# Moving pair 1's K transposes, a value load and a copy in the front of an attention and MLP kernel

## The chip, the cores and the metric

The kernel runs on one core of one Trainium2 chip. The metric is the device time of one execution in microseconds (us). The kernel before takes 340.07 us, the median of three runs (339.52 to 340.18).

The engines are TensorE (PE in the profile; PEld is its weight load), VectorE (DVE), ScalarE (ACT), GpSimd (POOL) and SyncE (SP). Each runs its own instructions in the order in which they were written, and waits on semaphores for the others. GpSimd and SyncE also issue the transfers (DMAs).

## The reference

Inputs are q, k and v with 8 batches, 8 heads, 576 positions and a head dimension of 64, a forget gate f per batch, head and position, and the two weights of an MLP (512 to 2048 to 512).

```python
scores = scale * np.matmul(q, k.transpose(0, 1, 3, 2))
log_f = np.log(np.clip(f, 0.0001, 1.0))
cum = np.cumsum(log_f, axis=-1)
decay = cum[:, :, :, None] - cum[:, :, None, :]
scores = np.where(causal, -1000000000.0, scores + decay)
attn = softmax(scores)          # written out in the reference
x = (attn @ v)                  # heads side by side: 4608 tokens of 512
h = x @ w_in
out = (h - np.tanh(h)) @ w_out
```

So each head has causal attention with a decay that is the difference of two running sums, and an MLP with the activation h - tanh(h) follows.

## The kernel before

**Pairs and tiles.** The work of attention is cut into 32 pairs of heads (4 pairs in each of 8 batches; pair 0 holds heads 0 and 1 of batch 0, pair 1 heads 2 and 3, and so on). A pair has seven score tiles (`TILES`), numbered 0 to 6. Tiles 0, 1, 2 are the first head's keys 0 to 511, tiles 4, 5, 6 the second head's. Tile 3, the tail tile, holds the last 64 keys of both heads: two small matmuls, one for each head. Scores are computed keys by queries, by `scores` (line 337): a matmul at line 352 from the transposed K (`KT`) and the transposed Q (`QT`), for batch 0 a second one at line 355 that adds the causal mask (`late`), and an exp on ScalarE (line 361). The decay is inside the matmul: `KT` and `QT` have 67 rows, 64 of the head dimension and 3 of the decay (constants, a high half `chi` and a low half `clo` of the running sum).

**The decay rows.** They are computed once: ScalarE takes the logarithm (line 184), VectorE the running sum (line 187), `chi` (line 189) and `clo` (line 190). For head 0 they are written directly. For heads 1 to 7 of batch 0 three DMAs on GpSimd's queue, at the top of `bulk` (lines 211 to 213: K's chi, Q's chi, K's clo), bring them into `KT` and `QT`.

**Loads.** Q, K and V are loaded on GpSimd's queue, with a cast to fp16: before `bulk` the first four heads of Q and K (lines 149 to 152, line 102), the last 64 positions of V (`load_v_rest`, line 123) and V of heads 0 and 1 (`load_v_head`, line 127, one DMA for each head); then the mask is made on GpSimd (line 169). `bulk` issues the decay rows, Q and K of heads 4 and 5, Q and K of heads 6 and 7, and V of heads 2 to 7 in four blocks (line 131). A DMA on this queue takes one of eight semaphores in turn, and so waits until the eighth before it has landed. Loads of batch 1 and of the weights (`load_win`, line 222, `load_wout`, line 226) follow from the table `LOADS` as the pairs go on.

**Transposes.** `trans` (line 287) turns a pair's Q or K on TensorE: six small transposes into one bank of the accumulator memory (line 298), and then two copies into `QT` or `KT`, even positions and odd positions. The string `copies` names the engine of each copy: "VV" puts both on VectorE (line 311), "AV" the first on ScalarE (line 309) and the second on VectorE. For pair 0 each copy is cut in two again.

**Banks.** Scores use the pool `ps_sc` (two banks in turn), and some of them the pool `ps_tr`, which has one bank, `tr`. In pair 0 the tail tile uses `tr`; in pair 1 tiles 0, 3 and 6 do. Transposes of the first pairs use three further banks in turn.

**Unread matmuls.** `unread(n)` (line 563) issues n matmuls of 128 columns whose result nobody reads, by default into `tr`.

**Order.** The order on each engine is written out by hand. `start` does pair 0's transposes and its tiles 0 and 1; `bulk` follows; then `att_items(p)` lists pair p's work, tile by tile. For pair 0: after the scores of tile 1 the transposes of pair 1's Q, after tile 2 six unread matmuls, after the scores of tile 3 the transposes of pair 1's K, after tile 5 four unread matmuls and after tile 6 six. During pair p the next pair's Q and K are turned (at `at_q` and `at_k`, line 614) and the values of the pair before are computed (`values`, line 382: the matmul of the exps with V at line 389, the first head at tile 2, the second at tile 4), divided on VectorE (lines 398 to 400). From pair 4 on matmuls of the MLP (line 451 and, later, 492 and 517) are mixed in. From batch 1 on the causal mask is applied by GpSimd behind the exp (line 371).

Of the kernel before, what the change touches and what calls it, by code (L numbers as in the profile page):

```python
# [21 lines left out]
def kernel(  # L22
# [18 lines left out]
    NPAIR = H // 2  # L41
# [51 lines left out]
    qn, kn = ([t[0:S // NT6, :].rearrange("p (h n d) -> p h n d", h=H, n=NT6) for t in raw] for raw in (qraw, kraw))  # L93
# [3 lines left out]
    KT = [qkp.tile([D + 3, H, PITCH], FP16, tag=f"KT{i}", name=f"KT{i}") for i in range(2)]  # L97
# [3 lines left out]
    def load_qk(dst, src, b, h0, h1):  # L101
        nc.gpsimd.dma_start(  # L102
            out=dst[b % 2][:, h0:h1, :, :].rearrange("p h n d -> p h (n d)"),
            in_=src[b, h0:h1, :, :].rearrange("h (p n) d -> p h (n d)", n=NT6))
# [21 lines left out]
    def load_v_head(b, h):  # L126
        nc.gpsimd.dma_start(out=vn[b % 2][:, 0:NJ - 1, h, 0:D],  # L127
                            in_=v[b, h, 0:S - S % P, :].rearrange("(n p) d -> p n d", p=P))

    def load_v_block(b, n, h0, h1):  # L130
        nc.gpsimd.dma_start(out=vn[b % 2][:, n, h0:h1, 0:D],  # L131
                            in_=v[b, h0:h1, n * P:(n + 1) * P, :].rearrange("h p d -> p h d"))
# [32 lines left out]
    EL = [cst.tile([P, 192], FP16, tag=f"el{i}", name=f"el{i}") for i in range(3)]  # L165
    load_v_rest(0)
    load_v_head(0, 0)
    load_v_head(0, 1)
    nc.gpsimd.affine_select(out=late, in_=late, compare_op=ALU.is_ge, fill=-60000.0,
                            base=0, pattern=[[1, P]], channel_multiplier=-1)  # L170

# [21 lines left out]
    def aug_rows(b):  # L193
        i, h0 = b % 2, 0 if b else 1
        hs = slice(b * H + h0, (b + 1) * H)
        return [(KT[i][D:D + 1, h0:H, 0:S], chi[hs, :]), (KT[i][D + 1:D + 2, h0:H, 0:S], clo[hs, :]), (QT[i][D + 2:D + 3, h0:H, :], chi[hs, :])]

    def load_aug(b):
        for to, of in aug_rows(b):
            nc.sync.dma_start(out=to, in_=of)  # L200

    def const_rows(i):
        h0 = 1 - i
        nc.sync.dma_start(out=QT[i][D:D + 2, h0:H, :], in_=minus16[0:2 * (H - h0), :])
        nc.sync.dma_start(out=KT[i][D + 2:D + 3, h0:H, 0:S], in_=ones16[0:H - h0, :])
# [3 lines left out]
    def bulk():  # L209
        (k_hi, chi_0), (k_lo, clo_0), (q_hi, _) = aug_rows(0)  # L210
        nc.gpsimd.dma_start(out=k_hi, in_=chi_0)
        nc.gpsimd.dma_start(out=q_hi, in_=chi_0)
        nc.gpsimd.dma_start(out=k_lo, in_=clo_0)
        load_qk(qn, q, 0, 4, 6)
        load_qk(kn, k, 0, 4, 6)
        load_qk(qn, q, 0, 6, H)
        load_qk(kn, k, 0, 6, H)
        for n in range(NJ - 1):
            load_v_block(0, n, 2, H)
# [22 lines left out]
    for b in range(2, B):  # L242
        p0 = (b - 1) * NPAIR
        at_q = [(p0 - 2, n + 2) for n in range(NJ)]
        at_k = [(p0, n) for n in range(NJ)]
# [4 lines left out]
        if b == FAR:  # L250
            at_q = [(p0 - 1, n + 1) for n in range(NJ)]
# [122 lines left out]
    AV = {}  # L374
# [216 lines left out]
    def att_items(p):  # L591
        def put(fn, *args):
            items.append((lambda: fn(*args), True))

        items = []
        here = pairs[p] if p < len(pairs) else None
        before = pairs[p - 1] if 0 < p <= len(pairs) else None
        after = pairs[p + 1] if p + 1 < len(pairs) else None
        early = p < NPAIR
        for ti in range(len(TILES)):  # L600
            if here and (p > 0 or ti > 1):
                put(scores, *here, ti)
            if p == 1 and ti == 6:
                items.append((lambda: const_rows(1), False))
                items.append((lambda: load_aug(1), False))
            if p == 0 and ti in (2, 5, 6):
                put(unread, {2: 6, 5: 4, 6: 6}[ti])
            if p == 1 and ti == 6:
                put(unread, 8, True)
            if p == 1 and ti == 3:  # L610
                put(last)
            for load in LOADS.get((p, ti), ()):
                items.append((load, False))
            at_q, at_k = (1, 3) if p == 0 else (0, 1) if early else (0, 2) if p == NPAIR else (0, 3)
            if p in (2 * NPAIR - 1, 2 * NPAIR, 2 * NPAIR + 1) and (ti % 2 or ti == 0):
                items.append((rest, False))
            if p in (2 * NPAIR - 1, 2 * NPAIR) and ti % 2 == 0:
                pair = pairs[2 * NPAIR + 2 * (p - 2 * NPAIR + 1) + ti // 4]
                put(trans, *pair, *((kn, KT) if ti % 4 else (qn, QT)), False, "VA")
            if ti == at_q and p < 2 * NPAIR - 1:  # L620
                put(trans, *after, qn, QT, early, "VV")
            if p == NPAIR:
                if ti in (4, 5):
                    put(mlp1, 0, ti - 4, 1)
            if ti == at_k and p < 2 * NPAIR - 1 and p != NPAIR:
                put(trans, *after, kn, KT, early, "AV" if early and p > 1 else "VV")
            if p == NPAIR:
                if ti == 1:
                    put(turn, *pairs[p - 2])
                    put(values, *before)  # L630
                    put(mlp1, 0, 0, 0)
                elif ti == 2:
                    put(mlp1, 0, 1, 0)
                    put(turn, *before)
                    put(trans, *after, kn, KT, early, "VV")
            elif early and ti in (2, 4) and before:
                put(values, *before, (ti // 2 - 1,))
            elif not early and ti == 2 and before:
                put(values, *before, (0, 1), p == NPAIR + 2)
            if p < NPAIR:  # L640
                if ti == 1 and p > 1:
                    put(turn, *pairs[p - 2], True)
            elif p > NPAIR and ti == 3:
                items.append((release, False))
                put(turn, *before)
        return items
# [5 lines left out]
    at = 0  # L652
    start()
    bulk()
    for p in range(len(pairs) + 1):
        b, c = divmod(p, NPAIR)
        items = att_items(p)
        take = TAKE[p] if p < len(TAKE) else 8 - (p - len(TAKE)) % 2
        if p == 2 * NPAIR - 1:
            keep()  # L660
        if p == 2 * NPAIR + 1:
            KEPT.clear()
            widen(1)
        mine = mlp[at:at + take]
        at += take
        first = 14 if p == NPAIR else 0
        if p == len(pairs):
            for fn, *args in mine[0:2]:
                fn(*args)
            mine = mine[2:]  # L670
        given, n = 0, 0
        whole = sum(counts for _, counts in items)
        for emit, counts in items:
            emit()
            n += counts
            while n > first and given < len(mine) and given * (whole - first) < (n - first) * len(mine):
                fn, *args = mine[given]
                fn(*args)
                given += 1
# [31 lines left out]
```

## Time and profile before

| what | before |
|---|---|
| median of three runs | 340.07 us |
| the profiled execution | 340.08 us, span 338.4 us |
| granted TensorE clock | 1.000 |
| TensorE busy | 331.6 us (98%) |
| VectorE busy | 261.1 us (77%) |
| ScalarE busy | 233.5 us (69%) |
| GpSimd busy | 162.6 us (48%) |
| DMA, mean | 115 GB/s |

Times in the profile are microseconds from the span's start. A line of a timeline gives the start, the duration, the engine, the line of the kernel, the operation, what it writes and reads, how many instructions are merged, and in brackets the idle time before it and what ended it. A line of the list of waits gives the engine and line that waited, what for, the sum in us, how often and the longest. A matmul's duration contains the time in which its results drain, so back-to-back matmuls overlap; their pace is read from their starts.

### The profile page before, as it was taken

Reading aid. Unit: us, or ns where it says so; the run is one execution under the profiler, and the core shown is the slowest. Engines: PE = TensorE matmul, PEld = TensorE weight load, DVE = VectorE, ACT = ScalarE, POOL = GpSimd, SP = SyncE. Lnnn points to the kernel's source line nnn. Section 1 sums busy time; section 2 is a strip of 40 time slices with the busy share of each in tenths; the row PEclk is TensorE's granted clock in tenths of the full one; section 3 lists DMA queues with packets and bytes.
Section 4 is the critical chain, followed back from the end, with each engine's and each line's share of the span. In section 5 each row is a group of like instructions: output and inputs, shape, how many; then the busy total and the mean of one; then the engine's idle time right before and its main releaser. Section 6 shows DMA issues by size and latency. Waiting matters only on the chain.

```text
span 338.4 us, 8760 instructions
## 1 busy us (share of the span) xinstructions
PE 331.6 (98%) x3329; PEld 237.4 (70%) x3329; DVE 261.1 (77%) x509; ACT 233.5 (69%) x438; POOL 162.6 (48%) x323
## 2 busy tenths in 40 slices
PE   8899999999999999999999999999999999999995
PEld 8675558875587558855888888656875686486485
DVE  7798986659888887678967796788667866966865
ACT  6798777888977886778677867787558733632630
POOL 8985566775657573677277637632322210000000
PEclk9999999999999999999999999999999999999999
DMA  8999999999969998999799999990130022002003
GB/s 110 130 196 198 186 198 177 182 157 171 138 92 169 143 132 90 135 175 146 96 120 175 132 112 113 166 131 17 50 110 8 17 67 95 2 31 95 0 17 110
DMA packets 147504, 38.82 MB, mean 115 GB/s; under 512 B 128217, under 2 KB 146371, under 8 KB 147462
## 3 DMA queue, kind: packets, MB, share of 16 engines
q0 software_dynamic: 94592, 18.38, 70.8%
q1 hardware_dynamic: 52864, 19.87, 33.2%
q8 instruction: 26, 0.43, 0.5%
q14 instruction: 16, 0.13, 0.2%
q10 hardware_dynamic: 6, 0.01, 0.0%
HBM read 36.85 MB, written 9.44 MB: 137 GB/s over the span
## 4 chain that ended last, share of the span: by engine, by line
PE 91%; DVE 2%; POOL 2%; ACT 2%; DMA 1%; issue 1%; ACTq 0%
PE hps L451 36%; PE ops L517 29%; PE ps L352 12%; PE av L389 8%; PE ops L492 4%; ACT e L361 2%; PE t L298 1%; DMA KT<-clo 1%; DVE KT L311 1%; DVE QT L311 0%; POOL vn L127 0%; POOL qn L102 0%; PE x L417 0%; POOL kn L102 0%; DVE xn L400 0%
## 5 line engine op out<-in xcount | busy, mean ns | idle before, releaser
L451 PE MATMUL hps<-XR,win 128*128 128x512 f16 (+1 forms) x640 | 140.7, 357 | 0.3 <-ACT XR L421 0.2
L456 ACT ACTIVATE th<-hps 128x512 f32<-128x512 f32 x144 | 86.6, 602 | 55.1 <-PE hps L451 53.5
L361 ACT ACTIVATE e<-ps 128x512 f16<-128x512 f32 x192 | 110.4, 598 | 9.6 <-PE ps L352 7.0
L462 DVE TENSOR_TENSOR gq<-hps,th 128x512 f16<-128x512 f32 x144 | 98.1, 687 | 23.5 <-ACT th L456 22.1
L371 POOL TENSOR_SCALAR_AFFINE_SELECT e<-e 128x128 f16<-128x128 f16 x168 | 59.2, 356 | 72.5 <-ACT e L361 70.5
L451 PEld LDWEIGHTS <-win 128*128 128x128 f16 x640 | 57.8, 97 | 48.6 <-issue 0.7
L352 PE MATMUL ps<-QT,KT 67*128 67x64 f16 (+4 forms) x384 | 76.5, 276 | 1.8 <-ACT e L361 0.6
L517 PEld LDWEIGHTS <-gq 128*128 128x128 f16 x640 | 60.3, 97 | 11.1
L517 PE MATMUL ops<-wout,gq 128*128 128x256 f16 x512 | 63.2, 272 | 0.0
L352 PEld LDWEIGHTS <-KT 67*128 67x128 f16 x384 | 36.5, 98 | 22.9 <-issue 1.3
L389 PEld LDWEIGHTS <-e 128*128 128x128 f16 x896 | 32.3, 97 | 3.6
L389 PE MATMUL av<-vn,e 128*128 128x65 f16 x896 | 33.6, 193 | 0.0
L131 POOL DMA_DIRECT2D vn<-in_v_dram x32 | 28.0, 879 | 7.1 <-DMA win<-in_moe_w_in_dram 3.3
L517 PE MATMUL ops<-W,sq 128*128 128x256 f16 x256 | 31.2, 272 | 0.0
L400 DVE TENSOR_TENSOR xn<-av,rs 128x640 f16<-128x640 f32 x32 | 26.4, 825 | 1.3 <-DVE rs L399 0.2
L517 PEld LDWEIGHTS <-sq 128*128 128x128 f16 x256 | 24.1, 98 | 3.4
L371 POOL TENSOR_SCALAR_AFFINE_SELECT el<-el 128x128 f16<-128x128 f16 x28 | 9.3, 332 | 26.8 <-ACT el L361 26.5
L108 POOL DMA_DIRECT2D qn<-in_q_dram x25 | 21.2, 846 | 1.8 <-issue 1.4
L108 POOL DMA_DIRECT2D kn<-in_k_dram x25 | 21.1, 846 | 1.7 <-issue 1.4
L398 DVE TENSOR_SCALAR rs<-av 128x10 f32<-128x10 f32 x32 | 5.2, 162 | 18.1 <-PE av L389 17.0
L311 DVE COPY KT<-t 64x576 f16<-64x576 f16 (+1 forms) x20 | 14.7, 736 | 3.7 <-PE t L298 3.5
L532 ACT ACTIVATE m<-ops 128x512 f32<-128x512 f32 x16 | 9.5, 596 | 10.9 <-PE ops L517 10.9
(85 smaller groups left out, 319.2 us busy)
## 6 DMA issues: line engine op xcount, KB each, us to landing
out_dram<-ost SPq DMA_DIRECT2D x34, 256.0 KB
vn<-in_v_dram POOLq DMA_DIRECT2D x24, 128.0 KB, 6.1
qn<-in_q_dram POOLq DMA_DIRECT2D x20, 128.0 KB, 4.6
kn<-in_k_dram POOLq DMA_DIRECT2D x20, 128.0 KB, 4.9
win<-in_moe_w_in_dram POOLq DMA_DIRECT2D x2, 1024.0 KB, 12.1
wout<-in_moe_w_out_dram POOLq DMA_DIRECT2D x2, 1024.0 KB, 15.7
XR<-xn SPq DMA_TRANSPOSE x56
qn<-in_q_dram POOLq DMA_DIRECT2D x6, 144.0 KB, 4.5
```

What stands on the lines that cost most here:

```text
L108: nc.gpsimd.dma_start(out=dst[b % 2][0:pn, n, :].rearrange("p (h d) -> p h d", h=H), in_=src[b, :, n * P:n * P + pn, :].rearrange("h p d - ...
L131: nc.gpsimd.dma_start(out=vn[b % 2][:, n, h0:h1, 0:D], in_=v[b, h0:h1, n * P:(n + 1) * P, :].rearrange("h p d -> p h d"))
L311: nc.vector.tensor_copy(out=to, in_=of)
L352: nc.tensor.matmul(out=ps[:, col:col + n], lhsT=kt[0:rows, h, j * P:(j + 1) * P], rhs=qt[0:rows, h, i0:i0 + n], start=True, stop=cut == 0)
L361: nc.scalar.activation(out=e[:, lo:hi], in_=ps[:, lo:hi], func=AF.Exp, bias=-SHIFT, scale=qscale)
L371: nc.gpsimd.affine_select(out=view, in_=view, compare_op=ALU.is_ge, fill=0.0, base=0, pattern=pat, channel_multiplier=-1)
L389: nc.tensor.matmul(out=av[:, a, ib, :], lhsT=E.pop((b, c, a, j, ib)), rhs=vn[b % 2][:, j, 2 * c + a, 0:D + 1], start=(j == 0), stop=(j == ib))
L400: nc.vector.tensor_tensor(out=xn.rearrange("p i (a d) -> p a i d", a=2), in0=av[:, :, :, 0:D], in1=rs.to_broadcast([P, 2, NJ, D]), op=ALU. ...
L451: nc.tensor.matmul(out=hps[:, o:o + n], lhsT=win[:, ci, ft * P:(ft + 1) * P], rhs=XR[:, ci, t:t + n], start=(ci == 0), stop=(ci == NCH - 1))
L456: nc.scalar.activation(out=th, in_=hps, func=AF.Tanh, scale=-1.0)
L462: nc.vector.tensor_tensor(out=GQ[(u, i)][:, half, kt, :], in0=hps, in1=th, op=ALU.add)
L517: nc.tensor.matmul(out=ps[:, m, :], lhsT=LHS[lhs](u, kt // 4)[:, kt % 4, m * P:(m + 1) * P], rhs=rhs[:, kt, :], start=(fresh and (apart or ...
```

## The change

Four things move. The V load of head 1 of batch 0 is issued in `bulk`, behind the decay rows and Q and K of heads 4 and 5, instead of ahead of the mask. During pair 0, pair 1's K is turned after tile 2 (behind its six unread matmuls) instead of after the scores of tile 3. The first half of its copy is done by ScalarE instead of VectorE ("AV"; K turned during pair 1 stays "VV", and K turned during pairs 2 and 3 was "AV" already). After tile 6 of pair 0 there are ten unread matmuls instead of six. On ScalarE the new copy stands between the exps of tile 2 and tile 3 of pair 0; VectorE's half waits for it.

Since one line goes and one comes, lines 169 to 214 of the kernel before have a number lower by one in the changed kernel.

```diff
     load_v_rest(0)
     load_v_head(0, 0)
-    load_v_head(0, 1)
     nc.gpsimd.affine_select(out=late, in_=late, compare_op=ALU.is_ge, fill=-60000.0,
...
         load_qk(qn, q, 0, 4, 6)
         load_qk(kn, k, 0, 4, 6)
+        load_v_head(0, 1)
         load_qk(qn, q, 0, 6, H)
...
             if p == 0 and ti in (2, 5, 6):
-                put(unread, {2: 6, 5: 4, 6: 6}[ti])
+                put(unread, {2: 6, 5: 4, 6: 10}[ti])
...
-            at_q, at_k = (1, 3) if p == 0 else (0, 1) if early else (0, 2) if p == NPAIR else (0, 3)
+            at_q, at_k = (1, 2) if p == 0 else (0, 1) if early else (0, 2) if p == NPAIR else (0, 3)
...
             if ti == at_k and p < 2 * NPAIR - 1 and p != NPAIR:
-                put(trans, *after, kn, KT, early, "AV" if early and p > 1 else "VV")
+                put(trans, *after, kn, KT, early, "AV" if early and p != 1 else "VV")
```

## The prediction

> **What bounds the kernel now.** I read the page first, then the list of TensorE's waits, then the chain of waits in the first 30 us, and last the timelines of the engines there. All durations are from the one profiled execution, which took 340.08 us (a span of 338.4 us and 1.68 us around it); the median of the three runs is 340.07 us (339.52 to 340.18), so the sum can be set against either.
>
> The page's busy times, its chain by engine, and then the whole list of TensorE's waits:
>
> ```profile
> PE 331.6 (98%) x3329; PEld 237.4 (70%) x3329; DVE 261.1 (77%) x509; ACT 233.5 (69%) x438; POOL 162.6 (48%) x323
> PE 91%; DVE 2%; POOL 2%; ACT 2%; DMA 1%; issue 1%; ACTq 0%
> PE idle L566 <- DVE warm L142: 1.1, 1, 1.1
> PE ps L352 <- ACT e L361: 0.6, 2, 0.4
> PE ps L352 <- DMA KT<-clo: 0.6, 1, 0.6
> PE hps L451 <- ACT XR L421: 0.2, 1, 0.2
> ```
>
> TensorE carries 91% of the chain and its listed waits come to 2.5 us in all; all lie before 32 us. Behind that it has no wait to lose. So the change can matter only by when the front of the kernel hands over, and a shift there goes to the end one for one.
>
> The chain, in order of time (start, duration, what), around the place of the change:
>
> ```profile
> 8.21 3.65 DMA KT<-clo
> 11.85 0.09 issue
> 11.94 0.19 PE ps L352
> ...
> 12.73 0.60 ACT e L361
> 13.34 0.04 issue
> 13.38 0.30 PE ps L352
> ...
> 13.88 0.35 PE idle L566 x6
> 14.23 0.04 issue
> 14.27 0.38 PE ps L352
> 14.65 0.06 PE ps L355
> 14.71 0.27 PE t L298 x6
> 14.98 0.02 issue
> 15.00 0.81 DVE QT L311
> ```
>
> A DMA (the decay rows of heads 1 to 7, clo last) lands at 11.85; the tail tile's second half waits for it (0.58 us); then ScalarE's exp of tile 4 holds tile 6 until 13.38; then come the unread matmuls, pair 1's tile 0 at 14.27, pair 2's Q transposes and, at 15.00, VectorE. From 15.00 to beyond 27 us VectorE copies and divides almost without a gap, and ScalarE has none from 18.88 to 28.7. So the start of VectorE's block at 15.00 sets all of the front.
>
> ScalarE, GpSimd and VectorE there (start, duration):
>
> ```profile
> 9.60 1.78 ACT L361 ACTIVATE e<-ps 128x512 f16<-128x512 f32 x3 [0.29 <-PE ps L355]
> 12.20 0.28 ACT L361 ACTIVATE el<-ps 128x128 f16<-128x128 f32 x1 [0.82 <-PE ps L355]
> 19.91 0.80 ACT L309 ACTIVATE KT<-t 64x576 f16<-64x576 f16 x1
> 4.97 1.54 POOL L127 DMA_DIRECT2D vn<-in_v_dram  x2
> 7.17 0.54 POOL L211 DMA_DIRECT2D KT<-chi  x1
> 12.46 1.62 DVE L311 COPY KT<-t 64x576 f16<-64x576 f16 x2 [0.59 <-PE t L298]
> ```
>
> ScalarE idles 0.82 us before the tail tile's exp: that is the hole in which the new copy can lie.
>
> **The change, part by part.**
>
> *Value load behind the decay rows.* It takes 0.77 us off GpSimd ahead of line 211 (half of 1.54). The mask would end at 6.25 instead of 7.02. But chi is written by VectorE only at 6.87 (line 189: 6.30 and 0.57), and SyncE's own issue from chi starts at 6.90, so line 211 starts at about 6.95 instead of 7.17. Lines 211, 212, 213 follow at 0.52 us each: clo's issue goes from 8.21 to about 8.0. The queue is also shorter by one load: neighbours land 0.65 to 0.7 us apart. Bounds for clo's landing: 11.85 (nothing gained) and 11.2 (all of 0.65); the smallest time from issue to landing in this queue is 3.5 us, so I take 11.5. Behind it, pair 2's loads are 0.2 us earlier, and everything from pair 3's Q on is issued 0.57 us later (0.77 less the 0.2). Slack: the moved load is issued near 9.8 and at 3.5 to 5.2 us lands by 15.0, wanted by the values at 16.5; pair 3's Q lands at 14.8 now, at most 15.5 then, wanted at 18.6; the last value block at 18.1, then 18.8, wanted at 20.3; w_in's first half at 27.5 (17.03 and 10.5), then at most 28.1, wanted at 28.7. GpSimd itself then waits for DMAs between 24.5 and 31.0, and its first mask of batch 1 at 31.82 stands 1.1 us of idle time ahead of need by 37.9. On SyncE nothing moves. Cost: nothing, unless w_in is more than a microsecond late.
>
> *Pair 1's K transposes ahead of the tail tile.* Six transposes take 0.26 us of TensorE either way. They go from 12.00 to right behind the unread matmuls, at about 10.94, and run to 11.35 with the drain (0.42). Their input lands at 8.67 (3.57 and 5.1). They fill a place where TensorE waited: tile 3 starts only at 11.14, when the unread matmuls in its bank have drained, and then stands for clo. New: tile 3's first half at 11.2, its second at about 11.6, tile 4 behind it done at about 12.1.
>
> *Half of the copy on ScalarE.* One L309 copy, 0.80 us by the row shown, is put on ScalarE between the exps of tile 2 (end 11.38) and of the tail tile. Packed closely, its successor started 0.67 us after it at 19.91. VectorE's half waits for ScalarE's and ends at about 13.05 (12.24 and 0.80); K was ready at 14.08 before, and is wanted by tile 0 at 14.1: hidden. ScalarE then runs: copy 11.40; tail exp from 12.07 to 12.20 (0.28 less overlap: 0.27); tile 4's exp from 12.34 to 12.47; its end 12.94 to 13.07, against 13.34 now. So tile 6 starts at 12.98 to 13.11 instead of 13.38: 0.27 to 0.40 us gained. That holds for any clo landing up to 11.7; at 11.85, 0.26 us is left. What is late next is ScalarE, which has become the bound of this stretch, so a still earlier clo buys nothing. Queued behind the copy are just those exps.
>
> *Four more unread matmuls.* Six take 0.50 us with their drain (13.72 to 14.22), eight 0.61 (line 566 at 17.61): 0.055 each, so four add 0.22. Tile 0 of pair 1 writes the same single bank, and now starts at 14.27, 0.05 behind the drain. Its K was ready at 14.08, and the chain names the unread matmuls. So all 0.22 us lies on the path. If it did not, the price would be zero; I take 0.22.
>
> *Sum.* 0.27 to 0.40 less 0.22: pair 1's tile 0 starts 0.05 to 0.18 us earlier; I take 0.15, as ScalarE packs its queue wherever its inputs are ready. VectorE's block then starts at 14.85 instead of 15.00. Nothing behind it is pinned to a DMA, so the end moves by 0.15: 340.08 - 0.15 = 339.93 us.
>
> *A rule weighed against the trace.* At the kernel's start 47 unread matmuls take 4.92 us, 105 ns each; from 5.9 us on they take 57 ns, and they stay so although TensorE stands still for 1.46 us between 10.0 and 13.4 (gaps of 0.19, 0.20, 0.74, 0.33 between issues). With the change I count 0.19 + 0.3 + 0.25 + 0.36 = 1.1 us. The Trainium skill's page "TensorE: Matmul & The Clock Gate", section "A second HAM failure mode: psum-queue depth-cycling", says that frequent short idling between groups of matmuls can drop the clock to half. By that rule the change could cost its rival below; by the row it costs nothing, since the gaps shrink.
>
> **The rivals.**
>
> *The whole stall goes.* If the unread drain did not hold tile 0 and the copy packed at 0.67, the gain would be 0.40 us or a little more: 339.6. For it: K waits on nothing else. Against it: both places with this bank (11.14, 14.27) show the drain. To pass 0.2% (0.68 us, about what a measurement of this kernel can tell from no change), tile 0 would have to start before 13.6, which ScalarE's copy and exps forbid; only a cause outside the front could give that.
>
> *The gain is eaten.* If clo lands no earlier and ScalarE takes longer over the copy while VectorE is busy in the same bank, tile 6 stays at 13.38 and the unread matmuls add 0.22: 340.3.
>
> *The clock falls.* The slower side. If the activity between 10 and 14 us falls below what holds full speed, the matmuls of pair 1 run at 105 instead of 57 ns. TensorE issues for some 3.7 of the 4.06 us between 14.27 and 18.33, so up to 3.7 us is lost, 1.5 if half of the stretch is hit: 341.6 to 343.8. It decides when the gaps exceed the 1.46 us that the clock now survives; my count is below. For it: the gaps lie differently. Against: a matmul pace of 57 ns throughout now.
>
> *A late load.* w_in a microsecond later than reckoned would hold line 451: 0 to 0.5 us, 340.1 to 340.4, since no more is in the queue shift.
>
> **How the numbers follow.** Forecast 0.50; whole stall gone 0.15; gain eaten 0.15; clock 0.05; late load 0.05; causes that I don't see 0.10, either way. The first three and the late load all stay within 0.2% (339.40 to 340.76) of 340.08 but for the spread of the runs: the lowest of three lies 0.56 us under the profiled one, and that on top of a gain of 0.15 to 0.4 crosses the line. So faster 0.17 (spread and unseen causes), same 0.68, slower 0.15 (clock 0.05, a late load or an eaten gain with something unseen 0.10). The range: below, 339.93 less 0.56 is 339.4, and 0.1 further for the larger gain, 339.3; above, the eaten gain at 340.3 with 0.3 for a late load, 340.6.
>
> **What would show it.** Right: clo lands near 11.5; a K copy on ScalarE at 11.4; the exp of tile 4 ends near 13.0; ten unread matmuls and pair 1's tile 0 at 14.1; VectorE's Q copy at 14.85. Wrong: tile 6 still at 13.38; a pace of 105 ns behind 10 us; a wait on w_in at line 451; or a front that hands over earlier than 0.2 us while the end does not follow.

## The result, and the profile after

The changed kernel takes 341.49 us, the median of 22 runs (339.86 to 344.57); the kernel before took 340.09 us in the same runs (22, 339.50 to 343.38). The ratio is 1.0047, with a 95% interval of 1.0027 to 1.0067: slower by 0.5%, where 339.93 us had been forecast. The spread is as telling as the median: the fastest run lies 0.2 us below the median of before, and half of the runs lie more than 1.4 us above it. Some runs, of the kernel before too, have a granted TensorE clock of 0.985 to 0.995 and lie between 341.5 and 344.6 us (two of the changed kernel's 22, four of e8's twelve below), but fifteen of the change's other twenty, at 0.999 or 1.000, lie above 341 us as well.

The profiled execution of the changed kernel took 342.32 us (span 340.6). Its busy times, its chain by engine and the whole list of TensorE's waits:

```profile
PE 332.2 (98%) x3333; PEld 237.5 (70%) x3333; DVE 261.2 (77%) x508; ACT 234.1 (69%) x439; POOL 165.5 (49%) x323
PE 84%; DVE 5%; DMA 3%; ACT 3%; SPq 2%; issue 1%; ACTq 0%; DVEq 0%
PE ops L517 <- DVE ost L536: 1.5, 1, 1.5
PE idle L566 <- DVE warm L142: 1.1, 1, 1.1
PE ps L352 <- DVE KT L120: 0.7, 1, 0.7
PE ps L352 <- ACT e L361: 0.4, 1, 0.4
PE hps L451 <- ACT XR L421: 0.2, 1, 0.2
PE ps L352 <- DVE KT L311: 0.2, 1, 0.2
```

The wait for clo (0.58 us) is gone, and so is one of the two waits for the exps. A small one for VectorE's copy of a K (0.2 us) has come, and two of 0.7 and 1.5 us on lines that the change does not touch. In the chain DMA has gone from 1% to 3%, and SyncE's queue (SPq) has entered it. The places of the two are in TensorE's timeline:

```profile
13.18 0.72 PE L566 MATMUL idle<-warm 128*128 128x128 f16 x10
13.95 0.38 PE L352 MATMUL ps<-QT,KT 67*128 67x512 f16 x1
...
96.74 0.39 PE L352 MATMUL ps<-QT,KT 67*128 67x512 f16 x1 [0.66 <-DVE KT L120]
...
108.24 1.03 PE L517 MATMUL ops<-wout,gq 128*128 128x256 f16 x8 [1.50 <-DVE ost L536]
```

Pair 1's tile 0 starts at 13.95, 0.32 us earlier than before. To see what became of that, I took the start of the same matmul (the first of the group in which the values of a pair read the tail tile's exp) in both traces, and the difference, after less before:

| time before, us | 16.10 | 28.22 | 47.61 | 72.95 | 82.17 | 91.40 | 99.91 | 108.41 | 275.24 |
|---|---|---|---|---|---|---|---|---|---|
| difference, us | -0.32 | -0.32 | -0.34 | -0.34 | -0.18 | -0.18 | +0.54 | +2.22 | +2.23 |

So the gain of the front holds to 73 us and is whole; 2.6 us are then lost between 73 and 108 us, and nothing after that. What is late there is a DMA. Batch 3 is the first whose K comes by another way: loaded in blocks by GpSimd (line 108), turned by DMA transposes that SyncE issues (line 113, into `TK`), and placed by VectorE (line 120). SyncE and VectorE of the changed kernel:

```profile
81.06 8.70 SPq L113 DMA_TRANSPOSE TK<-kn  x5
92.24 0.69 DVE L462 TENSOR_TENSOR gq<-hps,th 128x512 f16<-128x512 f32 x1 [0.73 <-ACT th L456]
96.23 0.45 DVE L120 COPY KT<-TK 64x1152 f16<-64x1152 f16 x1 [3.30 <-DMA TK<-kn]
96.60 0.15 DVE L398 TENSOR_SCALAR rs<-av 128x10 f32<-128x10 f32 x1
```

and of the kernel before, at the same place:

```profile
80.52 7.30 SPq L113 DMA_TRANSPOSE TK<-kn  x5
...
93.03 0.44 DVE L120 COPY KT<-TK 64x1152 f16<-64x1152 f16 x1
```

The five transposes were issued only half a microsecond later, but they landed 3.3 us too late. VectorE stands before line 120 for that time, and what is queued behind it (the divisions, the sums, the additions of line 536) is late in its turn: that is the second wait, at 108.24.

The loads ahead of them are late too. The landing of a few loads of GpSimd's queue (issue plus time to landing, which the profile gives in tenths), us:

| load | before: issued, landed | after: issued, landed |
|---|---|---|
| decay rows, K's clo | 8.21, 11.81 | 8.21, 11.41 |
| Q of heads 6 and 7 | 10.00, 14.80 | 10.77, 16.17 |
| w_in, first half | 17.03, 27.53 | 17.84, 28.44 |
| w_out, second half | 38.15, 56.55 | 37.88, 59.88 |
| batch 3's K, last block | 68.09, 72.79 | 70.60, 81.20 |
| batch 3's V, last block | 77.92, 82.12 | 77.73, 90.13 |

In the kernel before, the last K block lands 4.7 us after its issue, about as quickly as Q of heads 6 and 7 (4.8) and far from the 10.5 and 18.4 us of the weights: the queue has caught up by 73 us. In this execution of the changed kernel it is a microsecond behind at 28 us, 3.3 at 57, 8.4 at 81.

### The profile page after: what moved, and what is told of

It reads as the page before. It is cut to its first block, busy times and chain, and to the rows that moved or that the text cites. A ratio compares the mean times of both kernels' runs of the same rounds, so it can differ in the third digit from the quotient of the medians.

```text
span 340.6 us, 8768 instructions
## 1 busy us (share of the span) xinstructions
PE 332.2 (98%) x3333; PEld 237.5 (70%) x3333; DVE 261.2 (77%) x508; ACT 234.1 (69%) x439; POOL 165.5 (49%) x323
## 4 chain that ended last, share of the span: by engine, by line
PE 84%; DVE 5%; DMA 3%; ACT 3%; SPq 2%; issue 1%; ACTq 0%; DVEq 0%
PE hps L451 33%; PE ops L517 27%; PE ps L352 11%; PE av L389 7%; PE ops L492 4%; DMA TK<-kn 3%; ACT e L361 2%; SPq L113 2%; PE t L298 1%; DVE KT L311 1%; DVE gq L462 1%; DMA QT<-chi 1%; ACT th L456 0%; DVE QT L311 0%; DVE TQ L186 0%
## 5 line engine op out<-in xcount | busy, mean ns | idle before, releaser
L456 ACT ACTIVATE th<-hps 128x512 f32<-128x512 f32 x144 | 86.7, 602 | 55.2 <-PE hps L451 53.6
L371 POOL TENSOR_SCALAR_AFFINE_SELECT e<-e 128x128 f16<-128x128 f16 x168 | 61.3, 369 | 67.9 <-ACT e L361 66.2
L311 DVE COPY QT<-t 64x576 f16<-64x576 f16 x18 | 14.4, 800 | 3.9 <-PE t L298 3.8
L484 DVE TENSOR_TENSOR gq<-gq 128x512 f16<-128x512 f16 x32 | 17.1, 533 | 0.0
```

What stands on the lines that cost most here:

```text
L311: nc.vector.tensor_copy(out=to, in_=of)
L371: nc.gpsimd.affine_select(out=view, in_=view, compare_op=ALU.is_ge, fill=0.0, base=0, pattern=pat, channel_multiplier=-1)
L456: nc.scalar.activation(out=th, in_=hps, func=AF.Tanh, scale=-1.0)
```

## The experiments

Eighteen kernels were run, in five groups. Times are medians of 6 to 12 runs, with the range; in each group the kernel before was measured beside them (340.13, 340.11, 339.99, 340.04 and 340.09 us). The theory that I began with was the backlog that the moved value load leaves in the queue; the rival was that the order of the compute does it.

### The value load alone, the rest alone, a relief, and a delay

**e1**, the value load alone on the kernel before:

```diff
     load_v_head(0, 0)
-    load_v_head(0, 1)
...
         load_qk(kn, k, 0, 4, 6)
+        load_v_head(0, 1)
         load_qk(qn, q, 0, 6, H)
```

> The kernel before with the value load of head 1 put behind the decay rows, and nothing else. Theory (backlog): GpSimd idles 0.8 us for chi, its queue is fed less at 8 to 10 us, every load from pair 3's Q on lands 1.3 us later or more, and K of batch 3, which has no slack, is placed late by VectorE near 96 us. The loss is there without the other edits: 341.2 to 342.2 us, with the executions spread over 2 us or more, and a wait of TensorE on line 120 or 536 between 90 and 110 us. Rival (compute order): the loss comes from transposes, copy or unread matmuls that meet the transfers at another phase; then this kernel is at 339.8 to 340.2 with a narrow spread.

Measured: 339.86 us (339.64 to 340.86), ratio 0.9993 (0.9975 to 1.0011). The queue is behind as the theory said (Q of heads 6 and 7 lands at 15.07, w_in at 29.22), and in the profiled execution TensorE even waits 0.9 us for w_in; but the median shows no loss. The theory falls in this form.

**e2**, the changed kernel with the value load put back:

```diff
     load_v_head(0, 0)
+    load_v_head(0, 1)
...
         load_qk(kn, k, 0, 4, 6)
-        load_v_head(0, 1)
         load_qk(qn, q, 0, 6, H)
```

> The changed kernel with the value load of head 1 back ahead of the mask; K transposes ahead of the tail tile, ScalarE's copy and ten unread matmuls stay. Theory (backlog): the loss is gone; clo lands at 11.8 again and the front hands over 0.1 to 0.3 us earlier than before: 339.8 to 340.1 us with a narrow spread. Rival (compute order): 341 to 342 us as with the whole change.

Measured: 340.57 us (339.77 to 341.24), ratio 1.0012 (0.9992 to 1.0031). Between both expectations, and better than the change. Its front did not come out as expected: in the profiled execution (340.51) clo landed later than before, the tail tile's second half started at 12.04 (11.94 before), and the front hands over 0.07 us later than before instead of earlier; 0.3 us more is lost between 73 and 108 us.

**e3**, the changed kernel without one load:

```diff
-            add((p0, 5), load_qk, kn, k, b, 0, H)
```

> The changed kernel without the load of batch 2's K (1.2 MB read; batch 2 then uses the K of batch 0 that is left in the buffer, so the result differs and the work does not). Theory (backlog): the queue has 5 us of room before 60 us, the loads of batch 3 land in time, no wait of TensorE is left behind 32 us: 339.6 to 339.9 us, which is the 0.33 us that the front gained. Rival (compute order): the loss stays, above 341 us.

Measured: 340.00 us (339.78 to 341.00), ratio 0.9990 (0.9968 to 1.0013); the profiled execution took 339.79, and no wait of TensorE on a late transfer is in it. In that execution the front is 0.32 us ahead of before, and at 275 us it is still 0.29 ahead: with room in the queue the front's gain reaches the end. The median is that of the control below (e5), so as a gain in the median it is not shown.

**e4**, GpSimd held in the kernel before:

```diff
         load_qk(kn, k, 0, 4, 6)
+        nc.gpsimd.memset(hold, 0.0)
         load_qk(qn, q, 0, 6, H)
```

(`hold` is a tile that nothing reads; its definition is left out here.)

> The kernel before with a 0.8 us memset of an unused tile on GpSimd behind Q and K of heads 4 and 5, all loads in the old order. Theory (backlog) in its narrow form, that the late issue alone counts: loads from pair 3's Q on are issued 0.8 us later as with the change, and the kernel is at 341 to 342 us. In its other form, that the queue stood empty at 8 to 10 us because of the order: the queue is fed at that time as before, part of the 0.8 us is absorbed, 340.1 to 340.8 us. Rival (compute order): 340.1.

Measured: 340.43 us (339.76 to 343.25), ratio 1.0012 (0.9989 to 1.0036); the interval holds 1. It lies in the range of the second form of the theory. The profiled execution (341.01) waits 1.06 us for w_in.

### The control, the neighbours of the transposes, a later demand, another queue

**e5**, the kernel before without the load that e3 left out (the same line).

> The kernel before without the load of batch 2's K (batch 2 uses the K of batch 0 left in the buffer: other result, same work), the control for the changed kernel without it (340.0). If the kernel before loses nothing to late loads: 340.0 to 340.15 us, and the changed kernel's front then shows 0.1 to 0.3 us of gain in the difference of the two. If the queue also holds the kernel before: 339.7 to 339.9.

Measured: 340.01 us (339.56 to 340.70), ratio 0.9991 (0.9969 to 1.0013). The relief is worth 0.1 us before and 1.5 us after the change. So what the change loses is lost to the transfers. The other half of what was expected is missing: between this kernel and e3 there should be the 0.1 to 0.3 us of the front, and the medians are 340.01 and 340.00.

**e6**, the changed kernel without batch 3's V:

```diff
         for n in range(NJ):
-            if n < NJ - 1:
+            if b == FAR:
+                pass
+            elif n < NJ - 1:
                 add(at_v[n], load_v_block, b, n, 0, H)
```

> The changed kernel without the five loads of batch 3's V (batch 3 uses the V of batch 1 left in the buffer: other result, same work). They stand behind batch 3's K in the software queue and beside its DMA transposes. Theory (transposes share the engines with a backlog): the transposes of K at 81 to 90 us then land in 5 us as before, VectorE does not wait for them, 339.7 to 340.1 us. Rival (order of the queue): K itself is loaded late, as these loads stand behind it nothing changes, above 341 us.

Measured: 340.17 us (339.77 to 340.87), ratio 0.9997 (0.9974 to 1.0019). This profile can be set beside that of the changed kernel, since the lateness up to there is the same: the last K block lands at 81.28 (81.20 with the change). SyncE and VectorE of e6:

```profile
81.50 7.05 SPq L113 DMA_TRANSPOSE TK<-kn  x5
...
92.97 0.44 DVE L120 COPY KT<-TK 64x1152 f16<-64x1152 f16 x1
```

K is as late, its transposes are issued 0.4 us later still, and yet they land in time, with 7.05 us of issue instead of 8.70 and no wait of VectorE. So K's lateness in the queue is not enough: V's loads, which still move while the transposes run (the last lands at 90.13 with the change, at 82.12 before), are needed for the loss. They are not enough by themselves either. In e2 and in e13 (below) V's last block lands at 89.4 and 88.7 us, but K's last block at about 78, and VectorE waits for the transposes only this long:

```profile
94.12 0.45 DVE L120 COPY KT<-TK 64x1152 f16<-64x1152 f16 x1 [0.69 <-DMA TK<-kn]
93.64 0.45 DVE L120 COPY KT<-TK 64x1152 f16<-64x1152 f16 x1 [0.66 <-DMA TK<-kn]
```

So what is needed besides V's loads, and how they hold the transposes up, is not shown; K's lateness is a candidate, but in the two other traces with a long wait (e16 and e18) the landing of K's last block is not recorded.

**e7**, the demand later:

```diff
             if p == 1 and ti == 6:
-                put(unread, 8, True)
+                put(unread, 22, True)
```

> The changed kernel with 22 instead of 8 unread matmuls after tile 6 of pair 1: 0.8 us more on the path at 18 us, so that all behind it comes 0.8 us later against the transfers, as it did in the kernel with the value load alone, where TensorE waited 0.9 us for w_in. Theory (late loads are the whole of the loss, and a later demand takes as much of it back): 340.5 to 341.0 us, below the changed kernel's 341.5. Rival (the loss has nothing to do with when the loads are wanted): 342.2 us.

Measured: 340.80 us (340.11 to 341.38), ratio 1.0010 (0.9984 to 1.0036). Of the 0.8 us only 0.27 came onto the path (the rest lies beside VectorE's copy of pair 2's K), and the median is 0.7 us lower than with the change. That met the number of the theory, but not its arithmetic: 0.27 us of delay cannot give back 0.7 plus itself at one place.

**e8**, the decay rows on SyncE:

```diff
-        nc.gpsimd.dma_start(out=k_hi, in_=chi_0)
-        nc.gpsimd.dma_start(out=q_hi, in_=chi_0)
-        nc.gpsimd.dma_start(out=k_lo, in_=clo_0)
+        nc.sync.dma_start(out=k_hi, in_=chi_0)
+        nc.sync.dma_start(out=q_hi, in_=chi_0)
+        nc.sync.dma_start(out=k_lo, in_=clo_0)
```

with the value load back and six unread matmuls.

> A version meant to beat both: K transposes ahead and ScalarE's half copy as in the change, six unread matmuls, the value load back ahead of the mask, and the three decay row transfers of batch 0 issued by SyncE instead of GpSimd. GpSimd is 1.5 us freer ahead of Q and K of heads 4 and 5. Theory (backlog): the queue is fed earlier than before, no late load, clo lands by 10.5 us, the front hands over 0.4 to 0.6 us earlier: 339.4 to 339.7 us with a narrow spread. Rival (compute order): the K transposes and the copy cost here too, above 340.5.

Measured: 340.45 us (339.43 to 343.37), ratio 1.0019 (0.9990 to 1.0049). The loads are indeed earlier (Q of heads 6 and 7 lands at 13.36), but the rows are later: clo is issued at 8.38, and the tail tile's second half starts at 12.32. TensorE's list in this kernel:

```profile
PE ps L352 <- DMA KT<-clo: 0.9, 1, 0.9
PE ps L352 <- ACT e L361: 0.6, 2, 0.4
```

The version meant to beat both has a lower median than the change, but is not shown to beat the kernel before.

### Which of the parts

**e9** is the changed kernel again, without an edit.

> The changed kernel as it is, measured beside the three that follow. Theory: 341.0 to 342.0 us with a spread of 3 us or more, and where this profiled execution is slow, TensorE waits between 85 and 110 us for the placing of K (line 120) and VectorE's additions behind it. Rival (the first measurement met a chip or a time with slow transfers): below 340.5 us.

Measured: 341.96 us (340.06 to 344.54), ratio 1.0055 (1.0030 to 1.0081). The loss is there on both occasions. The profiled execution (340.36) is of the better ones and loses at another place, 0.6 us near 74 us, where the first lost 0.16:

```profile
74.34 0.38 PE L451 MATMUL hps<-XR,win 128*128 128x512 f16 x1 [0.43 <-DMA XR<-xn]
```

Again a DMA transpose that lands late, here of the MLP's input.

**e10**, the changed kernel with six unread matmuls:

```diff
-                put(unread, {2: 6, 5: 4, 6: 10}[ti])
+                put(unread, {2: 6, 5: 4, 6: 6}[ti])
```

> The changed kernel with six instead of ten unread matmuls: value load and K transposes moved, ScalarE's copy. Pair 1's tile 0 starts 0.22 us earlier than with the change. Theory (the value load puts the queue 1 us behind, and the earlier front asks for the loads sooner): the loss stays, 341.0 to 342.2 us. Rival (the unread matmuls are the cause): 339.5 to 339.7 us.

Measured: 339.92 us (339.56 to 341.23), ratio 0.9998 (0.9986 to 1.0010). My theory is not met; the rival's 339.5 to 339.7 is missed by 0.2 us, but the loss is gone, as it said. In its profile the front is 0.54 us ahead of before, so the four matmuls cost just 0.22 us where they stand, as reckoned; but they cost 1.6 to 2.0 us in the median. The front's 0.54 us reaches the end of this execution (0.51 at 275 us; 339.56 us).

**e11**, value load moved and ten unread matmuls, nothing else (the diffs of e1 and of the change).

> The kernel before with the value load moved and ten unread matmuls, K transposes and copies as before. The value load alone gave 339.86; four more unread matmuls give up 0.22 of its front. Theory (queue 1 us behind, whatever the compute order): 340.0 to 340.6. Rival (the ten unread matmuls make the loss, by the phase in which the later work meets the transfers): above 341 us.

Measured: 341.17 us (340.09 to 342.88), ratio 1.0032 (1.0009 to 1.0056): 1.3 us more than e1.

**e12**, K transposes and ScalarE's copy alone (e2 with six unread matmuls).

> K transposes ahead of the tail tile and ScalarE's half copy alone: value load and unread matmuls as before. Theory (the queue is not behind without the value load): clo at 11.8, tile 6 at 13.2, the front 0.2 to 0.35 us earlier than before, 339.75 to 339.95 us. Rival (the K transposes or the copy bring the loss): 340.6 or more, as with these and ten unread matmuls (340.57).

Measured: 339.84 us (339.60 to 340.22), ratio 0.9988 (0.9965 to 1.0010), and a narrow spread: 0.7 us less than with ten.

### Time or number

The four matmuls do two things: they hold the front up by 0.22 us, and they make TensorE's program longer by eight instructions (each matmul has its weight load). The last six runs part the two.

**e13**, the number with another place: eight instead of four after tile 5, six after tile 6.

```diff
-                put(unread, {2: 6, 5: 4, 6: 10}[ti])
+                put(unread, {2: 6, 5: 8, 6: 6}[ti])
```

> The changed kernel with six unread matmuls after tile 6 and eight instead of four after tile 5, where TensorE waits for ScalarE anyway: as many TensorE instructions as the changed kernel, the front as early as with six (0.54 us ahead of before). If the time at which the later work meets the transfers is what counts: 339.6 to 340.1 us. If the number of TensorE instructions counts: 341 to 342 us.

Measured: 342.25 us (340.07 to 343.60), ratio 1.0049 (1.0019 to 1.0079). The profiled execution is the fastest of the nine (340.07), and in it no wait of TensorE on a late transfer is listed; the same holds of e7 and e11. So no trace shows where the longer executions of these three lose their time.

**e14**, the time without the number: six unread matmuls, and ScalarE held ahead of the K copy.

```diff
+            if p == 0 and ti == 2:
+                put(pause)
```

(`pause` is one ScalarE copy of one element.)

> The changed kernel with six unread matmuls and one idle ScalarE operation of 0.2 us on one element ahead of the K copy: as many TensorE instructions as before, the front about 0.2 us later than with six, so some 0.33 us ahead of before, as with the whole change. If the time counts: 341 to 342 us with a wide spread. If the number of TensorE instructions counts: 339.75 to 340.2 us.

Measured: 340.06 us (339.74 to 341.21), ratio 0.9989 (0.9962 to 1.0017). The profiled execution (341.21) is the slowest of the eleven, and waits 1.40 us for w_in:

```profile
29.82 0.82 PE L451 MATMUL hps<-XR,win 128*128 128x512 f16 x3 [1.40 <-DMA win<-in_moe_w_in_dram]
```

**e15**, ten unread matmuls in the kernel before, nothing else.

> The kernel before with ten instead of six unread matmuls after tile 6 of pair 0, and nothing else: the front 0.22 us later. By their place on the path alone: 340.3 us with a narrow spread. If they cost more than their place, as in the three pairs measured: 340.8 to 342 us.

Measured: 340.55 us (340.24 to 344.40), ratio 1.0027 (1.0007 to 1.0047). The fastest run is at 340.24, the place alone; the median is 0.3 us above that, between the two expectations. Without the moved value load the extra cost is small.

**e16**, fourteen in the changed kernel.

> The changed kernel with 14 unread matmuls after tile 6: the front 0.22 us later again, 0.1 us ahead of before. If the loss grows with the number of TensorE instructions: above 342 us. If it comes and goes with the time at which the transfers are met: anything from 340.0 to 342, and a spread as narrow as before's is possible.

Measured: 342.45 us (340.66 to 344.18, 6 runs), ratio 1.0072 (1.0048 to 1.0096). The profiled execution has the same two waits as the first of the change:

```profile
PE ops L517 <- DVE ost L536: 1.5, 1, 1.5
PE ps L352 <- DVE KT L120: 0.9, 1, 0.9
```

**e17**, as e14 with three pauses.

> The changed kernel with six unread matmuls and three idle ScalarE operations ahead of the K copy (0.11 us each by the last run): TensorE instructions as before, the front 0.2 to 0.3 us ahead of before, later than with the whole change. If the time of the front counts: above 341 us. If the number of TensorE instructions counts: 339.8 to 340.4 us.

Measured: 340.12 us (340.08 to 340.86; eight of twelve runs between 340.10 and 340.12), ratio 0.9984 (0.9956 to 1.0011). The pauses cost more than I had reckoned, 0.56 us against e10, so the front stands where it stood before (+0.02 us).

**e18**, the number with a hidden place: six after tile 6 of pair 0, twelve instead of eight after tile 6 of pair 1.

> The changed kernel with six unread matmuls after tile 6 of pair 0 and twelve instead of eight after tile 6 of pair 1, where TensorE waits 0.25 us for VectorE's copy anyway: as many TensorE instructions as the change, the front 0.5 us ahead of before. If the number of TensorE instructions counts: 341 to 342.5 us with a wide spread. If the time of the front counts: 339.6 to 340.1 us.

Measured: 342.10 us (340.32 to 342.95), ratio 1.0023 (0.9987 to 1.0059), 2.2 us above e10 (339.92) by the medians; the wide interval, which holds 1, comes from the kernel before in that group. Ten of its twelve runs lie above 341 us; none of e17's twelve, taken beside them, does. The profiled execution (342.09) shows

```profile
96.03 0.45 DVE L120 COPY KT<-TK 64x1152 f16<-64x1152 f16 x1 [3.05 <-DMA TK<-kn]
```

In the profiles of e13 and e18 the front was 0.35 and 0.34 us ahead, not the 0.54 that I had expected (in one the first transposes began later, in the other clo landed later), so single executions do not settle the time. Set side by side the medians say more. All of these have the value load moved, unless marked; the front is that of the profiled execution:

| front, us against before | TensorE instructions as before | eight or more added |
|---|---|---|
| about -0.5 | e10: 339.92, e1: 339.86 | |
| -0.44 | e14: 340.06 | |
| -0.30 to -0.35 | e12 (load not moved): 339.84 | the change: 341.49, 341.96; e13: 342.25; e18: 342.10 |
| -0.1 | | e16 (16 added): 342.45 |
| about 0 | e17: 340.12 | e11: 341.17; e7 (36 added): 340.80 |

With the load moved, and e3 and e6 with their missing loads aside, the kernels with the longer TensorE program have medians of 340.80 to 342.45, those with the old one 339.86 to 340.12, with the front from 0.5 us ahead to where it was. Two kernels with the front at the same place, e17 and e11, lie 1.05 us apart. So the loss goes with the added instructions and not with the time of the front. Two limits: at -0.30 to -0.35 there is no kernel with the load moved and the old program, only e14 and e17 on either side; and the loss does not grow with the number, as e7 adds most and loses least. How the added instructions reach the transposes is not shown.

One candidate can be looked at: the transfers that the page of the profile calls instruction.

```profile
q8 instruction: 26, 0.43, 0.5%
q14 instruction: 16, 0.13, 0.2%
```

The 26 packets of q8, of about 16 kB each (0.43 MB by 26), come to one for every 256 of the 6658 matmuls and weight loads of TensorE, so I take them for TensorE's program; the trace does not name the engine. Each keeps one DMA engine busy for 0.9 to 2.2 us, some in the midst of the transposes. If their place made the loss, the one between 80 and 90 us would move with the number of instructions. In eleven traces it seems to: it starts at 83.6 to 85.8 in five kernels with the old number (before, e10, e12, e14, e17) and at 86.7 to 87.4 in six with more (the change twice, e11, e13, e16, e18). But in six of the other nine it does not: at 86.7 and 86.1 in e1 and e4, with the old number, and at 83.5, 83.8, 83.6 and 84.2 in e3, e6, e7 and e15, with more. In all twenty it goes with V's loads instead: it starts by 84.5 where V's last block lands by 83.8 us or V is not loaded, and at 85.5 to 87.4 where it lands at 85.2 or later (in e16, where that landing is not recorded, the block before lands at 88.0). So the packet's place follows the backlog and not the number of instructions; that it makes the loss is not shown.

## Why the prediction was wrong, point by point

- **What bounds the kernel.** That the front's handing over sets the end one for one, since "Behind that it has no wait to lose", is the step that failed, with its form in the sum: "Nothing behind it is pinned to a DMA". What the runs showed in its place: in the profiled execution the front's 0.32 us was whole at 73 us, then the DMA transposes of batch 3's K landed so late that VectorE waited 3.3 us for them and TensorE 0.66 and 1.50, and the end came 2.2 us later than before. One for one does hold where no transfer is late (e10: 0.54 at the front, 0.51 at 275 us; e12: 0.30 and 0.28). A list without waits says that nothing was late in that execution. It does not say by how little. K of batch 3 was placed at 93.03 before, wanted by TensorE at about 96, behind loads that stay backlogged to 70 us; that should have been measured transfer by transfer, as it was for w_in.
- **The front.** Right in mechanism, and mis-sized: 0.15 us forecast, 0.30 to 0.32 measured in the two profiles of the change. The term is ScalarE's. The copy stood at 11.37, the tail tile's exp at 12.05, and tile 4's exp at 12.20, 0.15 behind it where 0.27 had been taken (the profile before has both: an exp of the tail tile and the next start 0.27 apart at 21.11 and 0.15 at 25.17); so tile 6 started at 12.84 instead of 12.98 to 13.11. VectorE's block began at 14.68 (14.85 forecast). VectorE's half of the copy was hidden, as said.
- **The value load.** chi's DMA was issued at 7.17 as before, not at 6.95: GpSimd waited for it in both kernels, 0.82 us now. clo landed at 11.41 (11.5 forecast) with its issue unmoved; one load less ahead of it is the likely cause. What stands behind was issued 0.77 us later, not 0.57, and landed later than the bounds given: Q of heads 6 and 7 at 16.17 against at most 15.5, w_in's first half at 28.44 (29.22 in e1) against at most 28.1. "Cost: nothing, unless w_in is more than a microsecond late": by itself that held in the median (e1), although w_in was late enough in some executions.
- **Four more unread matmuls.** 0.22 us on the path: exactly that (0.32 against 0.54). But their price is not their place on the path. With the moved value load they cost 1.3 to 2.0 us in the median, without it 0.5 to 0.7 (0.22 of each is the place). No row of the profile before shows it. It comes with added TensorE instructions, wherever they stand in the front, and its way to the transfers is open.
- **The rivals.** "The clock falls" did not come: ten unread matmuls still end within 0.72 us, and the mean granted clock of the profiled executions is 0.998 to 1.000. (Its price was also too high: 3.7 us of matmuls at 105 instead of 57 ns would cost 3.1 us more, not 3.7.) The rule of the Trainium skill (the page "TensorE: Matmul & The Clock Gate", the section on psum-queue depth-cycling) therefore did not bite here, with gaps of about 1.0 us between its issues from 10 to 13.4 us, where I had counted 1.1. "A late load" was the right family at the wrong address: I had priced w_in at up to 0.5 us, and it cost 0.94 and 1.40 us in single executions of e1 and e14; the changed kernel lost at transposes that I had not looked at (2.6 us in the profiled execution).
- **The range.** Its upper end, 340.6, was built from a single late load. Slower had 0.15.

## What to carry to other kernels

Where transfers are backlogged over a long stretch of the kernel, a list of waits that is empty is no slack: write down for each late-needed transfer when it landed and when it was wanted, and treat a queue that has just caught up as a bound. When a stretch with DMA transposes follows, look at what is loaded beside them as well as at when their own input lands: here a late input alone cost no wait (e6). A filler instruction that is cheap where it stands should be tested with its place and its number apart, and over a dozen runs, because one profiled execution can miss the loss: one of the change was 0.3 us slower than that of before, another 2.2.

## What the runs showed that was not expected

- With the value load moved, eight TensorE instructions more, wherever they stood in the first 18 us, cost 1.1 to 2.3 us in the median and spread the runs over 2.5 us or more; delays made by ScalarE did not.
- The DMA transposes of K were slower beside loads: five took 8.70 us to issue and kept VectorE waiting 3.3 us with V's loads beside them, 7.05 us and no wait without, with K equally late. With V as late and K 3 us less late the wait was 0.7 us (e2, e13).
- In one trace each, small transfers issued by SyncE were no quicker than GpSimd's: clo, issued at 8.38, let the tail tile go at 12.32; issued by GpSimd at 8.21, behind a queue of loads, it had landed by 11.81.
- None of the kernels is shown to beat the one before: the lowest medians, 339.84 (K transposes and copy alone) and 339.86 (value load alone), have intervals that hold 1. Both halves of the change without the additional unread matmuls gave 339.92, which holds 1 as well.
